# Two more pairs of a chunked state-space kernel transposed by DMA, and two stores issued by GpSimd

## The chip, the cores and the metric

The kernel runs on one core of a Trainium2 chip. The metric is the device time of one execution in microseconds; lower is better. The time before is the median of three runs. TensorE (PE in the profile), VectorE (DVE), ScalarE (ACT) and GpSimd (POOL) compute; SyncE (SP) only issues DMAs, and GpSimd and ScalarE can issue them too. Each engine works through its own instructions in order.

## The reference

Two stages, one behind the other. The first is a Mamba2-style scan over 4 batches, 8 heads and 768 positions, with head width 32 and state width 16, in chunks:

```python
L = np.exp(cum[:, :, :, None] - cum[:, :, None, :]) * causal
CB = np.einsum('bhin,bhjn->bhij', Cc, Bc)
y_intra = np.einsum('bhij,bhjd->bhid', CB * L, xc)
y_inter = np.einsum('bhin,bhnd->bhid', Cc, state) * decay_to_i
state = decay_full * state + sum_j(Bc x xc * decay_from_j)
```

Its result, as 3072 tokens of 256 features, goes through a gated feed-forward stage:

```python
gate = np.maximum(x @ w_gate, 0.0)      # 256 -> 1536
out = (gate * (x @ w_val)) @ w_out      # 1536 -> 256, float32
```

## The kernel before

The decays are folded into B and C: each position's B and C are multiplied by a factor (`fac`), so that within a chunk the product C·B already carries L, and only the causal mask is left. Chunks are 128 positions here, and two chunks of one batch with all 8 heads make a **pair**; there are 12 pairs (0 to 11). Two pairs make a **block** of 512 tokens for the feed-forward stage; the blocks of the outer loop are `b` = 0 to 5. While block b runs its feed-forward matmuls (`gv`, `gvh`, `fout`), the scan of later pairs is threaded between them: `P = 2b+2`, `Q = 2b+3`, `W = 2b+1`. The order on each engine is the order of the program text (`in_order` pins it), so what stands ahead of a waiting instruction on an engine, or behind it, can be read off the code.

For a pair p the steps are:

- `load(p)` or `held(p)`: SyncE loads C and B (`load_bc`, two DMAs each, L92) into `bcr`, and x (`load_x`, two DMAs, L100) into `xr`. `held` first writes one element with VectorE, which ties the load to VectorE's progress.
- `scale(p)`: B and C times `fac`, cast to bf16, on GpSimd, and `to_x(p)`: x cast to bf16 (`xb`, L318).
- A transpose of B and C, so that the state index n lies on the partitions. Pairs 0 to 5: scaled values go to `bs` (`scale_bc` L344, or `scale_one` L353 for one of B and C), `turn(p)` transposes them on TensorE (four matmuls against the identity, L389) into PSUM, and `tevac(p)` copies them out: B to `BT` on ScalarE, and C twice to `CT`, each time with the rows of half of the heads zeroed by `tmask` (L415 on VectorE). Pairs 6 to 11 (`NDMA = 6`): `scale_padded` writes B and C into one of three tiles `bz` (list `turned`, index p % 3), which were zeroed once, in eight slots of 128 columns; per chunk i, slot 4i is B, 4i+1 is C, and 4i+2 and 4i+3 are C with half of the heads left zero (L297, L303). One DMA transpose by SyncE (L306) then turns the whole tile into `TT`.
- `G(p)`: C·B for both chunks and all heads (L452, reading `BT` and `CT`); `G_rows` (L491) does so from `TT` for pairs 6 to 11. `gevac(p)`: two of the four quarters of the result leave PSUM through ScalarE (L464, L472) and get the causal mask from GpSimd (`affine_select`, L171); the rest is masked by VectorE (L475, L479).
- `inter(p, i)`: the carried state times C (L619, reading `CT` through `ct`); `Dm(p)`: the masked C·B times x (L630; for two pairs `Dm_two`, L678). `states(p)` (L569) and `states_two` (L693): B times x, summed over chunks; `spread` prepares it for `inter`.
- `yevac` writes the result to `yT`, which the feed-forward stage reads.

`foevac(b, ts)` (L811) copies a block's output to `ob` on ScalarE and stores it; every block's stores but the last ones are issued by SyncE (L814).

At the change, the program before reads as follows. End of block 0: `held(5)` (C, B and x of pair 5 on SyncE, L1064), the scan steps of pairs 2 and 3, `scale_one(4)` for B on GpSimd (L1117), the second store of block 0. Start of block 1 (L966): `load(6)`, `load(7)` on SyncE. Inside it: `states(4)` and `scale_one(4)` for C (L989); from f = 6 on `turn(4)`, `tevac(4)`, `scale(5)` (L1017); from f = 8 on `turn(5)`, `tevac(5)`, `scale(6)`, `load(8)` (L1021); then `inter(4)`, `fout(1, 0)`, `G(4)` with its masks, `Dm(4)`, `states(5)`, `G(5)`. Block 2 works on pairs 6 and 7 with `G_rows` and `Dm_two`, while GpSimd scales pairs 8 and 9.

Of the kernel before, what the change touches and what calls it, by code (L numbers as in the profile page):

```python
# [11 lines left out]
ALU = mybir.AluOpType  # L12
# [17 lines left out]
def kernel(  # L30
# [13 lines left out]
    nc = tc.nc  # L44

    NB, NH, S, D = x.shape
    N = B.shape[-1]
# [23 lines left out]
    NWIDE = 4  # L71
# [220 lines left out]
    def scale_padded(p, eng):  # L292

        b, c0, _ = place(p)
        z = turned[p % 3]
        f = fac[:, b, c0:c0 + 2].rearrange("s i j h -> s i (j h)")
        eng.tensor_tensor(  # L297
            out=z.rearrange("s (i k) (h n) -> s i (k h) n", k=4, n=N)[:, :, 0:2 * NH],
            in0=st[p]["bcr"].rearrange("s i j h n -> s i (j h) n"),
            in1=f.to_broadcast([128, 2, 2 * NH, N]), op=ALU.mult)  # L300
        parts = z.rearrange("s (i k) (q t n) -> s i k t q n", k=4, q=4, t=2)
        for t in range(2):
            eng.tensor_copy(out=parts[:, :, 2 + t, t], in_=parts[:, :, 1, t])  # L303
        st[p]["B"] = [z[:, 4 * i] for i in range(2)]
        tt = st[p]["TT"] = att.tile([128, 8, 128], BF16, tag="TT", name="TT", bufs=4)
        nc.sync.dma_start_transpose(out=tt, in_=z.rearrange("s k n -> s (k n)"))  # L306

    def new_bs(p):
        st[p]["bs"] = att.tile([128, 4, 128], BF16, tag="bs", name="bs", bufs=6)
# [107 lines left out]
    def ct(p, i, rows=slice(0, 128), t=None):  # L417
        if p < NWIDE:
            c = st[p]["CT"][rows, :, :, 64 * i:64 * i + 64]
        else:  # L420
            c = st[p]["CT"][rows, :, i]
        return c if t is None else c[:, t]

    def split(p, ap):

        return ap.rearrange("s t (r m) -> s t r m", r=2) if p < NWIDE else ap
# [17 lines left out]
    def G(p):  # L444
        s = st[p]
        if "gp" not in s:
            G_banks(p)
        g = s["gp"]
        for i in range(2):
            for q in range(4):  # L450
                r = slice(32 * q, 32 * q + 32)
                nc.tensor.matmul(  # L452
                    out=split(p, g[q][:, i]), lhsT=s["BT"][r, i], rhs=ct(p, i, r),
                    start=(i == 0), stop=True, tile_position=(32 * q, 0),
                    skip_group_check=True)
        s["gs"] = att.tile([128, 4, 4, 128], BF16, tag="gs", name="gs", bufs=2)
# [344 lines left out]
    def foevac(b, ts, o=None):  # L801
        last = b == NBLK - 1 and ts == 2
        if ts % 2 == 0 and not last:
            return
        ob = ffn.tile([128, 2, DM], FP32, tag="ob", name="ob", bufs=3)
        r0 = b * 512 + ts * 128
        if last:
            nc.scalar.copy(out=ob[:, 0], in_=fst["o"][:, 0])
            nc.scalar.dma_start(out=out[r0:r0 + 128, :], in_=ob[:, 0])
            return  # L810
        nc.scalar.copy(out=ob, in_=o or fst["o"])  # L811
        rows = out[r0 - 128:r0 + 128, :].rearrange("(i p) m -> p i m", p=128)
        for part in ((slice(0, 1), slice(1, 2)) if b in (2, 3) and ts == 3 else (slice(0, 2),)):
            nc.sync.dma_start(out=rows[:, part], in_=ob[:, part])  # L814


    B_, C_ = slice(0, 1), slice(1, 2)
# [89 lines left out]
    def turn(p):  # L907
        transp(p, 1)
        transp(p, 0)
# [53 lines left out]
    for b in range(NBLK):  # L963
        P, Q, W = 2 * b + 2, 2 * b + 3, 2 * b + 1
        more = P < NPAIR
        if b == 1:  # L966
            load(P + 2, nc.sync)
            load(P + 3, nc.sync)
        if b == 2:
            scale(Q, nc.gpsimd)  # L970
            load(Q + 2, nc.sync)

        nh = (4, 6, 8, 0)[min(b, 3)]
        for f in range(nh):
            if b == 0:
                continue
            turning = f == (3 if b == 1 else nh - 3)
            gvh_mm(b, f, 0)
            gvh_relu(b, f, 0)
            gvh_mul(b, f, 0)  # L980
            if b == 1 and f == 1:
                to_x(P, nc.scalar)
            if turning:
                inter(W, 0)
                inter(W, 1)
                Dm(W)
                if b == 1:
                    states(P)
                    scale_one(P, nc.gpsimd, 1)  # L989
                else:  # L990
                    states_two((P, Q))
                yevac(W, nc.scalar)
                if b == 1:
                    spread(P)
                else:
                    sums_two((P, Q))
# [4 lines left out]
        for f in range(nh, NF):  # L1001
            gv(b, f, b > 2 and f == 0)
            if b == 0:
                if f == 5:
                    over_sum(de_ps)
                if f == 7:
                    sevac(1, 1)
                if f == 9:
                    turn(P)
                    tevac(P, nc.scalar, nc.vector)  # L1010
                if f == 10:
                    held(Q, bc=False)
                if f == 11:
                    back(P)
                    backevac(P, nc.scalar)
            elif b == 1:
                if f == nh:  # L1017
                    turn(P)
                    tevac(P, nc.scalar, nc.vector)
                    scale(Q, nc.gpsimd)  # L1020
                if f == 8:  # L1021
                    turn(Q)
                    tevac(Q, nc.scalar, nc.vector)
                    scale(Q + 1, nc.gpsimd)
                    load(Q + 3, nc.sync)
            elif b == 2:
                if f == 9:
                    scale(Q + 2, nc.gpsimd)
                    load(Q + 3, nc.sync)
                    load(Q + 4, nc.sync)  # L1030
            elif b == 3:
                if f in (2, 6):
                    scale(P + 2 + f // 4, nc.gpsimd)
# [3 lines left out]
        if b == 0:  # L1037

            for third in range(3):
                fs = range(4 * third, 4 * third + 4)  # L1040
                fout(b, 0, fs)
                fout(b, 1, fs)
                if third == 0:
                    new_bc(Q + 1)
                    nc.vector.memset(st[Q + 1]["bcr"][0:1, 0, 0, 0, 0:1], 0.0)
                    load_bc(Q + 1, 0, nc.sync)
                    new_x(Q + 1)
                    for i in range(2):
                        load_x(Q + 1, i, nc.sync)
                    load_bc(Q + 1, 1, nc.sync)  # L1050
                    for n in range(1, NB):
                        nc.vector.reciprocal(fac[:, n, :, 0], fac[:, n, :, 1])
                if third == 0:
                    turn(Q)
                if third == 1:
                    G(P)
                    gevac(P)
                    tevac(Q, nc.scalar, nc.vector)
            foevac(b, 1)
            to_x(Q, nc.scalar)  # L1060
            fout(b, 2)
            state(P, 0)
            state(P, 1)
            held(Q + 2)  # L1064
            back(Q)
            backevac(Q, nc.vector)
            fout(b, 3, range(6))
            inter(P, 0)
            inter(P, 1)
        elif b == 1:  # L1070
            fout(b, 0)
            G(P)
            gevac(P)
            over_sum2(de)
            fout(b, 1)
            foevac(b, 1)
            fout(b, 2)
        elif more:
            ahead = (P + 2, Q + 2) if Q + 2 < NPAIR else ()
            fout(b, 0, range(9), True)  # L1080
            G_rows(P)
            opened = y_banks()
            inter_rows(P, opened)
            inter_rows(Q, opened)
            gevac(P)
            fout(b, 0, range(9, NF))
            fout(b, 1)
            first_two = fst["o"]
            fout(b, 2, range(1))
            G_rows(Q)  # L1090
            gevac(Q)
            foevac(b, 1, first_two)
            fout(b, 2, range(1, NF))
            fout(b, 3, range(8))
            Dm_two((P, Q))
            states_two(ahead)
            yevac_two((P, Q))
            sums_two(ahead)
            fout(b, 3, range(8, NF))
            foevac(b, 3)  # L1100
            continue
        else:
            fout(b, 0)
            fout(b, 1)
            foevac(b, 1)
            fout(b, 2)
            foevac(b, 2)
            fout_last(b)
            continue
        Dm(P)  # L1110
        states(Q)
        if b == 0:
            yevac(P, nc.vector)
            G(Q)
            gevac(Q, after={3: lambda: spread(Q)})
            new_bs(Q + 1)
            scale_one(Q + 1, nc.gpsimd, 0)  # L1117
        else:
            yevac(P, nc.scalar)
            G(Q)  # L1120
            spread(Q)
            gevac(Q)
# [34 lines left out]
```

## Time and profile before

| | us |
|---|---|
| median of three runs (122.37 to 123.28) | 122.76 |
| the profiled execution's own time | 122.67 |
| its span in the trace | 121.0 |

| engine | busy us | share of the span |
|---|---|---|
| TensorE, matmuls | 115.5 | 95% |
| VectorE | 89.0 | 74% |
| ScalarE | 74.3 | 61% |
| GpSimd | 51.5 | 43% |

The granted TensorE clock is 1.0 over the whole span. Where the profile's text gives times, they count from the start of the span. "L306" is line 306 of the kernel before. Names such as `TT<-bz` mean "writes TT, reads bz". SPq rows are SyncE's DMA issues: their length is the time in which SyncE was busy issuing, not the time of the transfer; the time from issue to landing is given separately. The waits shown in brackets are the idle time of an engine ahead of an instruction and who ended it.

### The profile page before, as it was taken

How to read it: one execution, taken by the hardware profiler on the slowest of the kernel's cores; microseconds unless marked ns; L12 is line 12 of the kernel's file. 1: busy time of each engine (PE TensorE's matmuls, PEld its weight loads, DVE VectorE, ACT ScalarE, POOL GpSimd, SP SyncE). 2: the span in 40 equal slices, each digit the busy share in tenths (PEclk: the TensorE clock that was granted, in tenths of full speed). 3: DMA queues.
4: the chain of work that ended last, by engine and by line, in shares of the span. 5: the costliest groups of instructions: out<-in, count | busy, mean ns of one | idle time of the engine just before them, and what ended most of it. 6: DMA issues, size and time to landing. Idle time of an engine off the chain costs nothing.

```text
span 121.0 us, 3322 instructions
## 1 busy us (share of the span) xinstructions
PE 115.5 (95%) x1231; PEld 74.8 (62%) x1238; DVE 89.0 (74%) x214; ACT 74.3 (61%) x161; POOL 51.5 (43%) x104
## 2 busy tenths in 40 slices
PE   7789999999999999999999999999999999999990
PEld 2245864577885477888487544578444677444790
DVE  5888888977999956899875687866778675678500
ACT  4166886843998744888734767525767445766340
POOL 6879999831705252857084363433400033000000
PEclk9999999999999999999999999999999999999999
DMA  3999999999989999899978799962200002200022
GB/s 67 208 172 162 201 186 188 207 141 130 161 99 170 125 105 131 106 202 182 115 138 136 80 107 152 197 127 78 95 5 0 0 0 92 87 0 0 0 87 87
DMA packets 80591, 13.69 MB, mean 113 GB/s; under 512 B 73424, under 2 KB 80576, under 8 KB 80576
## 3 DMA queue, kind: packets, MB, share of 16 engines
q1 hardware_dynamic: 73088, 10.54, 56.9%
q0 software_dynamic: 4080, 2.36, 14.0%
q10 hardware_dynamic: 3408, 0.59, 2.6%
q8 instruction: 9, 0.15, 0.5%
q14 instruction: 6, 0.05, 0.1%
HBM read 11.12 MB, written 3.15 MB: 118 GB/s over the span
## 4 chain that ended last, share of the span: by engine, by line
PE 89%; DVE 3%; DMA 3%; issue 1%; SPq 1%; ACT 0%; DVEq 0%
PE o L783 26%; PE gate L738 19%; PE val L738 19%; PE gv L753 13%; DMA bcr<-in_C_dram 3%; PE g L452 2%; PE g L491 2%; PE y L678 1%; PE y L630 1%; PE o L795 1%; DVE bs L344 1%; PE tp L389 1%; DVE gs L475 1%; PE y L619 1%; PE y L665 0%
## 5 line engine op out<-in xcount | busy, mean ns | idle before, releaser
L742 DVE TENSOR_TENSOR h<-r,val 128x512 bf16<-128x512 bf16 x54 | 36.7, 686 | 9.3 <-ACT r L741 6.4
L741 ACT ACTIVATE r<-gate 128x512 bf16<-128x512 f32 x54 | 32.3, 597 | 11.9 <-PE gate L738 10.9
L783 PE MATMUL o<-wo,h 128*128 128x256 bf16 x276 | 33.7, 273 | 0.0
L738 PE MATMUL gate<-yT,wg 128*128 128x512 bf16 x105 | 32.0, 379 | 0.2
L738 PE MATMUL val<-yT,wv 128*128 128x512 bf16 x105 | 31.5, 379 | 0.2
L783 PEld LDWEIGHTS <-h 128*128 128x128 bf16 x276 | 25.7, 98 | 5.6 <-issue 1.4
L171 POOL TENSOR_SCALAR_AFFINE_SELECT gs<-gs 128x512 bf16<-128x512 bf16 (+1 forms) x24 | 12.2, 531 | 25.3 <-ACT gs L464 25.3
L475 DVE TENSOR_TENSOR gs<-g,masks 128x512 bf16<-128x512 f32 x24 | 15.4, 684 | 6.3 <-PE g L491 2.8
L738 PEld LDWEIGHTS <-wv 128*128 128x128 bf16 x108 | 10.6, 98 | 12.5
L738 PEld LDWEIGHTS <-wg 128*128 128x128 bf16 x108 | 10.4, 98 | 11.1
L464 ACT CAST gs<-g 128x512 bf16<-128x512 f32 x12 | 7.0, 587 | 14.6 <-PE g L452 6.2
L763 DVE TENSOR_TENSOR h<-r,gv 128x256 bf16<-128x256 bf16 x36 | 13.9, 416 | 0.9 <-ACT r L760 0.7
L760 ACT ACTIVATE r<-gv 128x256 bf16<-128x256 f32 x36 | 13.7, 389 | 1.2
L753 PE MATMUL gv<-yT,wg 128*128 128x256 bf16 x72 | 13.9, 273 | 0.0
L753 PE MATMUL gv<-yT,wv 128*128 128x256 bf16 x72 | 13.9, 273 | 0.0
L297 POOL TENSOR_TENSOR bz<-bcr,fac 128x512 bf16<-128x512 f32 x6 | 6.3, 1058 | 9.1 <-DMA bcr<-in_B_dram 9.1
L811 ACT COPY ob<-o 128x512 f32<-128x512 f32 x11 | 6.5, 595 | 4.0 <-PE o L783 4.0
L318 ACT CAST yT<-y 128x512 bf16<-128x512 f32 (+1 forms) x9 | 4.6, 531 | 5.4 <-PE y L678 3.4
L753 PEld LDWEIGHTS <-wv 128*128 128x128 bf16 x72 | 7.0, 98 | 0.8
L753 PEld LDWEIGHTS <-wg 128*128 128x128 bf16 x72 | 6.8, 98 | 1.1 <-issue 0.2
L318 POOL CAST xb<-xr 128x512 bf16<-128x512 f32 (+1 forms) x9 | 5.3, 594 | 3.8 <-DMA xr<-in_x_dram 3.7
L318 DVE CAST yT<-y 128x256 bf16<-128x256 f32 (+1 forms) x7 | 3.7, 550 | 4.0 <-PE y L678 2.0
(119 smaller groups left out, 110.7 us busy)
## 6 DMA issues: line engine op xcount, KB each, us to landing
xr<-in_x_dram SPq DMA_DIRECT2D x23, 128.0 KB, 3.3
out_dram<-ob SPq DMA_DIRECT2D x9, 256.0 KB, 2.5
bcr<-in_B_dram SPq DMA_DIRECT2D x16, 64.0 KB, 3.0
bcr<-in_C_dram SPq DMA_DIRECT2D x16, 64.0 KB, 2.9
wg<-in_moe_w_gate_dram POOLq DMA_DIRECT2D x6, 128.0 KB, 4.8
wv<-in_moe_w_val_dram POOLq DMA_DIRECT2D x6, 128.0 KB, 5.0
wo<-in_moe_w_out_dram POOLq DMA_DIRECT2D x3, 256.0 KB, 7.1
out_dram<-ob SPq DMA_DIRECT2D x4, 128.0 KB, 2.4
```

What stands on the lines that cost most here:

```text
L171: nc.gpsimd.affine_select(out=dst, in_=dst, pattern=pattern, compare_op=ALU.is_ge, fill=0.0, base=0, channel_multiplier=-1)
L318: (eng.copy if eng is nc.scalar else eng.tensor_copy)(out=out, in_=in_)
L464: nc.scalar.copy(out=d[:, 0], in_=g[0])
L475: nc.vector.tensor_tensor(out=d[:, q], in0=g[q], in1=m, op=ALU.mult)
L738: nc.tensor.matmul(out=o, lhsT=w_tile(ws, f, k), rhs=yT[:, k, tk], start=(k == 0), stop=(k == 1), skip_group_check=True)
L741: nc.scalar.activation(r, g, AF.Relu)
L742: nc.vector.tensor_tensor(out=fst[b][:, f], in0=r, in1=v, op=ALU.mult)
L753: nc.tensor.matmul(out=gv_[:, j], lhsT=w_tile((wgs, wvs)[j], f, k), rhs=yT[:, k, tk], start=(k == 0 and not (early and j)), stop=(k == 1), ...
L760: nc.scalar.activation(r[:, 0:256], fst[b, f, u][:, 0], AF.Relu)
L763: nc.vector.tensor_tensor(out=fst[b][:, f, u * 256:(u + 1) * 256], in0=fst.pop((b, f, u, "r"))[:, 0:256], in1=fst.pop((b, f, u))[:, 1], op ...
L783: nc.tensor.matmul(out=o[:, ts % 2], lhsT=fst[b][:, f, ts * 128:(ts + 1) * 128], rhs=wo[:, f], start=(f == 0 and new), stop=(f == NF - 1), ...
L811: nc.scalar.copy(out=ob, in_=o or fst["o"])
```

## The change

Pairs 4 and 5 take the DMA way. A new function `scale_turned(p)` writes B and the two half-zero forms of C, scaled, straight into the padded tile (four GpSimd instructions, no plain C in slot 4i+1), and `turn_padded(p)`, split off from `scale_padded`, issues the DMA transpose. `ct` and `G` read `TT` for these pairs; their matmuls keep their shapes. The transposes, copies and `bs` tiles of the two pairs are gone.

The order of SyncE's queue changes. Before: C and B of pair 5, x of 5, a store, C and B of pair 6, x of 6, load of 7, transpose of 6. After: C and B of 5, transpose of 4, x of 5, C and B of 6, transpose of 5, x of 6, load of 7, transpose of 6. On GpSimd: the masks of pair 2, the first store of block 0, the masks of pair 3, `scale_turned(4)`, the second store of block 0, `scale_turned(5)`, `to_x(5)`, and then the scaling of pair 6 as before.

```diff
@@ scale_padded
         st[p]["B"] = [z[:, 4 * i] for i in range(2)]
+        turn_padded(p)
+
+    def scale_turned(p, eng):
+
+        b, c0, _ = place(p)
+        z = turned[p % 3]
+        dst = z.rearrange("s (i k) (q t n) -> s i k t q n", k=4, q=4, t=2)
+        src = st[p]["bcr"].rearrange("s i j (t q) n -> s i j t q n", t=2)
+        f = fac[:, b, c0:c0 + 2]
+        for j in range(2):
+            for t in range(2):
+                eng.tensor_tensor(
+                    out=dst[:, :, j * (2 + t), t], in0=src[:, :, j, t],
+                    in1=f[:, :, j, 4 * t:4 * t + 4].to_broadcast([128, 2, 4, N]), op=ALU.mult)
+        st[p]["B"] = [z[:, 4 * i] for i in range(2)]
+
+    def turn_padded(p):
         tt = st[p]["TT"] = att.tile([128, 8, 128], BF16, tag="TT", name="TT", bufs=4)
-        nc.sync.dma_start_transpose(out=tt, in_=z.rearrange("s k n -> s (k n)"))
+        nc.sync.dma_start_transpose(out=tt, in_=turned[p % 3].rearrange("s k n -> s (k n)"))
@@ ct
-            c = st[p]["CT"][rows, :, i]
+            c = st[p]["TT"][rows, 4 * i + 2:4 * i + 4]
@@ G
-                    out=split(p, g[q][:, i]), lhsT=s["BT"][r, i], rhs=ct(p, i, r),
+                    out=split(p, g[q][:, i]), rhs=ct(p, i, r),
+                    lhsT=s["BT"][r, i] if p < NWIDE else s["TT"][r, 4 * i],
@@ foevac
-            nc.sync.dma_start(out=rows[:, part], in_=ob[:, part])
+            (nc.sync if b else nc.gpsimd).dma_start(out=rows[:, part], in_=ob[:, part])
@@ the loop over blocks
         if b == 1:
-            load(P + 2, nc.sync)
+            new_bc(P + 2)
+            load_bc(P + 2, 1, nc.sync)
+            load_bc(P + 2, 0, nc.sync)
+            scale_turned(Q, nc.gpsimd)
+            turn_padded(Q)
+            new_x(P + 2)
+            for i in range(2):
+                load_x(P + 2, i, nc.sync)
             load(P + 3, nc.sync)
+            to_x(Q, nc.gpsimd)
...
                     states(P)
-                    scale_one(P, nc.gpsimd, 1)
...
             elif b == 1:
-                if f == nh:
-                    turn(P)
-                    tevac(P, nc.scalar, nc.vector)
-                    scale(Q, nc.gpsimd)
                 if f == 8:
-                    turn(Q)
-                    tevac(Q, nc.scalar, nc.vector)
                     scale(Q + 1, nc.gpsimd)
                     load(Q + 3, nc.sync)
...
-            held(Q + 2)
+            held(Q + 2, with_x=False)
...
-            new_bs(Q + 1)
-            scale_one(Q + 1, nc.gpsimd, 0)
+            scale_turned(Q + 1, nc.gpsimd)
+            turn_padded(Q + 1)
+            new_x(Q + 2)
+            for i in range(2):
+                load_x(Q + 2, i, nc.sync)
```

## The prediction

> **What bounds the kernel now.** I read the busy shares first, then the chain of waits, then the order of the SyncE queue and of GpSimd where the change falls, and last the DMA view. One profiled execution: span 121.0 us, its own time 122.67 us, so 1.67 us lie outside the span. The median of the three runs is 122.76 us, 0.09 above it. The runs reach from 122.37 to 123.28, so about 1% (1.2 us) is what a measurement tells from no change.
>
> ```profile
> PE 115.5 (95%) x1231; PEld 74.8 (62%) x1238; DVE 89.0 (74%) x214; ACT 74.3 (61%) x161; POOL 51.5 (43%) x104
> ```
> ```profile
> PE 89%; DVE 3%; DMA 3%; issue 1%; SPq 1%; ACT 0%; DVEq 0%
> PE o L783 26%; PE gate L738 19%; PE val L738 19%; PE gv L753 13%; DMA bcr<-in_C_dram 3%; PE g L452 2%; PE g L491 2%; PE y L678 1%; PE y L630 1%; PE o L795 1%; DVE bs L344 1%; PE tp L389 1%; DVE gs L475 1%; PE y L619 1%; PE y L665 0%
> ```
>
> The chain is TensorE almost throughout; ScalarE has 0% of it. So a microsecond off TensorE's stream is a microsecond off the end, as long as nothing that feeds it turns late. The second view to read is therefore what feeds it:
>
> ```profile
> DMA  3999999999989999899978799962200002200022
> ```
>
> The DMA engines are full until about two thirds of the span, and the change adds DMA work in that part.
>
> **What comes off TensorE.** The chain of waits of the stretch where pairs 4 and 5 are turned, and where their results are first read (start us, us, what):
>
> ```profile
> 37.81 0.22 PE tp L389 x4
> 39.76 0.22 PE tp L389 x4
> 42.57 0.22 PE y L619 x4
> ```
>
> The eight transposes stand on the chain with 0.22 + 0.22 = 0.44 us, between matmuls that follow without a gap. They go. The two copies on ScalarE and the four masked copies on VectorE that emptied them go too; the chain shows these engines hardly at all, so I cost their going at nothing, below and above. Matmuls of G and of the inter term for pairs 4 and 5 read TT in place of BT and CT with the same shapes: nothing. Without any new wait the kernel is at 122.67 - 0.44 = 122.23.
>
> **What is added to SyncE's queue.** Its rows before (start us, us, line, tile, count):
>
> ```profile
> 29.90 0.83 SPq L814 DMA_DIRECT2D out_dram<-ob  x1
> 30.83 1.19 SPq L92 DMA_DIRECT2D bcr<-in_C_dram  x2
> 32.07 1.41 SPq L92 DMA_DIRECT2D bcr<-in_B_dram  x2
> 33.52 2.52 SPq L100 DMA_DIRECT2D xr<-in_x_dram  x2
> 36.14 0.53 SPq L814 DMA_DIRECT2D out_dram<-ob  x1
> 36.77 1.18 SPq L92 DMA_DIRECT2D bcr<-in_C_dram  x2
> 38.00 1.28 SPq L92 DMA_DIRECT2D bcr<-in_B_dram  x2
> 39.38 1.38 SPq L100 DMA_DIRECT2D xr<-in_x_dram  x2
> 40.80 1.64 SPq L92 DMA_DIRECT2D bcr<-in_C_dram  x2
> 42.49 1.36 SPq L92 DMA_DIRECT2D bcr<-in_B_dram  x2
> 45.19 1.46 SPq L306 DMA_TRANSPOSE TT<-bz  x1
> 46.71 2.12 SPq L92 DMA_DIRECT2D bcr<-in_C_dram  x2
> 48.87 1.54 SPq L92 DMA_DIRECT2D bcr<-in_B_dram  x2
> 53.20 1.30 SPq L306 DMA_TRANSPOSE TT<-bz  x1
> 54.56 2.28 SPq L92 DMA_DIRECT2D bcr<-in_C_dram  x2
> ```
> ```profile
> L306 SPq DMA_TRANSPOSE TT<-bz x6: 1233/1442/1537, 45.2 to 77.1; - x6
> DMA to landing us min/median/max: 2.7/3.9/5.1
> ```
>
> SyncE issues one DMA after the other with no room between, so whatever is put into the queue moves every later load. I call the shift of the loads s and add it up to the B load of pair 9.
> - Issue: two transposes at the median 1.44 make +2.9; the two stores that leave took 0.83 + 0.53 = 1.36. Net +1.5.
> - New wait: the transpose of pair 4 waits for GpSimd's scaling, and x of pair 5, B and C of pair 6, the transpose of pair 5 and all behind them queue with it. SyncE gets there at 33.48 less 0.93 for the store, 32.55. GpSimd is done with the four scaling instructions at 33.38 (row below: the four instructions of the same size, 31.89 to 33.38). So +0.8.
> - Eased congestion: x of pair 5 took 2.52 where x of pair 6 took 1.38, 1.1 more with no transpose near. A pause of SyncE just ahead lets the engines catch up: between 0 and -1.1, and I take -1.1, since the pause stands right in front of it.
> - What a transpose leaves behind it: C and B after the transpose at 45.19 took 3.66 together; those of pairs 6 and 7 took 2.46 and 3.00. That is +0.9, and C behind the one at 53.20 shows the same. Two of these are 0 to 1.8. But the 1.1 at 33.52 says that such hold-ups come without transposes, so I take half of one, 0.45.
>
> Likeliest s = 1.5 + 0.8 - 1.1 + 0.45 = 1.65, with ends 0.4 (1.5 - 1.1) and 4.1 (1.5 + 0.8 + 1.8).
>
> The transposes' own landing is covered: that of pair 4 is issued at about 33.4 and at the longest landing, 5.1, is there at 38.5, ahead of its first reader at 42.57 less 0.44. That of pair 5, issued near 40 and landed by 45.1, is read by G(5), which stands between the two Dm rows below, after 47.0.
>
> **What is added to GpSimd.** Its rows (start, us, line, tile, count, [idle before and releaser]):
>
> ```profile
> 30.89 1.04 POOL L171 TENSOR_SCALAR_AFFINE_SELECT gs<-gs 128x512 bf16<-128x512 bf16 x2 [3.24 <-ACT gs L464]
> 31.89 1.49 POOL L353 TENSOR_TENSOR bs<-bcr,fac 128x128 bf16<-128x128 f32 x4
> 43.27 0.61 POOL L318 CAST xb<-xr 128x512 bf16<-128x512 f32 x1
> 45.18 1.00 POOL L171 TENSOR_SCALAR_AFFINE_SELECT gs<-gs 128x512 bf16<-128x512 bf16 x2 [1.29 <-ACT gs L464]
> 60.72 1.06 POOL L297 TENSOR_TENSOR bz<-bcr,fac 128x512 bf16<-128x512 f32 x1 [3.86 <-DMA bcr<-in_B_dram]
> 62.38 0.61 POOL L318 CAST xb<-xr 128x512 bf16<-128x512 f32 x1
> 62.95 1.01 POOL L171 TENSOR_SCALAR_AFFINE_SELECT gs<-gs 128x512 bf16<-128x512 bf16 x2
> 64.96 1.00 POOL L171 TENSOR_SCALAR_AFFINE_SELECT gs<-gs 128x512 bf16<-128x512 bf16 x2 [1.00 <-ACT gs L464]
> ```
> ```profile
> L153 POOL DMA_DIRECT2D wg<-in_moe_w_gate_dram x6 | 4.6, 774 | 0.3 <-POOL wg L225 0.3
> ```
>
> A store issued here is not in the trace; the nearest row is a weight load issued by GpSimd, 0.77 us. The first one falls into the 3.24 us of idle time before 30.89, the second behind the scaling of pair 4, in front of that of pair 5, whose data is what it waits for anyway. Both at nothing; were that cover gone, 0.77 us would go onto s, inside its upper end. B of pair 4 is ready after two of the four instructions, 32.7, as before, so the states of pair 4 do not move.
>
> **Where s meets TensorE.** GpSimd works in order, and behind the load waits stand the causal masks that the Dm matmuls read:
>
> ```profile
> 47.09 0.41 PE L630 MATMUL y<-gs,xb 128*32 128x128 bf16 x16
> 66.32 0.63 PE L678 MATMUL y<-gs,xb 128*32 128x128 bf16 x32
> ```
> ```profile
> DMA to landing us min/median/max: 3.0/3.1/3.2
> ```
>
> First place: x of pair 6 (landing line above: the pair of x loads issued at 39.38, whose second lands near 43.2) lets the cast start at 43.27, then 1.0 us of mask for pair 4. With s it ends at 43.27 + 0.61 + 1.0 + s = 44.9 + s, and Dm(4) wants it at 47.09 - 0.44 = 46.65: covered to s = 1.8. Second place: GpSimd stood 3.86 us waiting for B of pair 9; from 60.72 on it scales, copies, casts and masks without a pause until 63.96, then the second mask takes 1.0. That ends at 64.96 + s, and the Dm of pairs 6 and 7 wants it at 66.32 - 0.44 = 65.9: covered to s = 0.9. This is the tighter place. A stall at the first gives the second the same time more, so the larger of the two counts, not the sum: the uncovered part is s - 0.9.
>
> So the sum is 122.67 - 0.44 + (1.65 - 0.9) = 123.0.
>
> **A rule on the stores.** The DMA share by windows (last but one column; busy us of each engine before it):
>
> ```profile
> 36.80:45.20 8.40, 8.35 (x65) 4.95 (x64) 6.58 (x14) 5.53 (x12) 4.01 (x8) 1.00 1.04 140
> ```
>
> With a share of 1.04 the 16 engines themselves may set the pace, and not SyncE's issuing. Then moving the stores frees nothing: s = 1.65 + 1.36 = 3.0, uncovered 2.1, time 124.3. The Trainium skill, page "DMA: Bandwidth & Descriptors", section "Issuing engines are not separate DMA queues", says that DMAs started from the scalar, sync or gpsimd queue share the same 16 engines, and that spreading them over queues only saves time on the sequencer. The share agrees with that as far as it goes; that the rows behind the queue come at 0.6 us each whatever their bytes speaks for SyncE as the pace.
>
> **The rivals.**
> - Forecast: TensorE gains 0.44, the loads shift by 0.9 to 2.65, part of it is uncovered. 122.2 to 124.0, likeliest 123.0. Chance 0.52.
> - All covered: s at most 0.9, because the removed stores and the eased congestion pay for the transposes. 122.2, chance 0.18. For it: 1.5 - 1.1. Against it: one more wait on GpSimd.
> - Slower: the load stream is held up, and the Dm matmuls of pairs 6 and 7 wait for a mask behind B of pair 9. It decides for over 1% from s = 2.65. By the engines as the pace, 124.3 (chance 0.12); by hold-ups behind both transposes, up to s = 4.1, 125.4 (chance 0.14). For it speaks the DMA view of 45 to 53 us, where in 0.2 us slices the data stops for about 1.4 us after the transpose was issued:
>
> ```profile
> GB/s 119 103 102 100 125 183 214 201 202 241 261 266 58 0 0 3 6 10 10 9 210 293 198 145 141 123 124 70 62 59 56 92 120 118 127 153 150 168 151 139
> ```
>
> - Faster by over 1%: 1.2 us would have to go where the chain shows 0.44. I see no row for the rest. Chance 0.04.
> - That the change does not do what it says I leave out: the eight transposes are gone from TensorE's order in the changed program.
>
> **The numbers.** Faster by over 1% 0.04; within 1% 0.52 + 0.18 = 0.70; slower 0.26. Time 123.0, the likeliest case. The range starts at 122.0 (all covered, less a little scatter of the runs) and ends at 124.6: it takes in the engine-paced case and leaves out the worse half of the slower one and the faster one, 0.16 together.
>
> **What would show it.** Right: no tp rows on the chain between 36 and 42 us; SyncE reaching x of pair 6 later by 1 to 2 us than 39.38; GpSimd's scaling of pair 9 later than 60.72 by about s, and an idle time of TensorE of under a microsecond before the Dm of pairs 6 and 7, released by GpSimd. Wrong: no TensorE idle there (all covered); one of 2 us or more, or one already at Dm(4) (held up); or a wait at states of pair 4 or at the inter term of pair 4, which would mean that the scaling or the new transpose itself is late.

## The result and the profile after

The changed kernel takes 124.31 us (median of six runs, 123.67 to 126.42), the kernel before beside it 122.75 us (six runs, 122.37 to 123.37). The ratio is 1.0105, with a 95% interval of 1.0076 to 1.0134: slower by about 1%. (The ratio leaves out executions more than 1.5% above the fastest of their kernel, here two of the six, and the medians do not, so the medians lie further apart.) The forecast was 123.0 with a range of 122.0 to 124.6. The time is inside the range, near the figure of the case that was called slower, and on the edge of what had been called "within 1%".

The profiled execution of the changed kernel took 123.67 us, the fastest of its six and 1.00 more than that of before (122.67); its span is 122.0 us. First the busy shares and the chain of waits of the page after:

```profile
PE 116.8 (96%) x1223; PEld 75.1 (62%) x1230; DVE 88.1 (72%) x210; ACT 73.6 (60%) x159; POOL 53.3 (44%) x108
```
```profile
PE 69%; DMA 10%; POOL 7%; SPq 6%; DVE 3%; issue 2%; ACT 1%; POOLq 0%; ACTq 0%; DVEq 0%
PE o L801 17%; PE gate L756 16%; PE val L756 15%; PE gv L771 7%; DMA bcr<-in_B_dram 5%; DMA xr<-in_x_dram 5%; PE w L200 4%; SPq L92 3%; POOL gs L171 3%; SPq L323 2%; POOL bz L297 2%; PE y L696 1%; PE g L469 1%; PE g L509 1%; PE o L813 1%
```

TensorE's share of the chain fell from 89% to 69%. DMA, GpSimd and SyncE together now hold 23%, where the chain of before had 4% of DMA and SyncE and no GpSimd. TensorE's busy sum looks no smaller (116.8 against 115.5), although it has eight instructions fewer: its ends are modelled, and a matmul that waits inside a group counts as busy. So the sum can't show the gain; the starts of groups can.

TensorE's rows at the three places that matter, after (start us, us; the bracket is the idle time ahead). The first row is the first gate matmul of block 0; the same row starts at 16.17 in the kernel before:

```profile
16.14 0.38 PE L756 MATMUL gate<-yT,wg 128*128 128x512 bf16 x1
...
47.21 0.71 PE L648 MATMUL y<-gs,xb 128*32 128x128 bf16 x16 [0.52 <-POOL gs L171]
...
66.74 1.21 PE L696 MATMUL y<-gs,xb 128*32 128x128 bf16 x32
```

Read against the gate row, Dm of pair 4 starts at 31.07, before at 47.09 - 16.17 = 30.92. Eight transposes are gone in between (0.44), so it waited 0.15 + 0.44 = 0.59 (the bracket names 0.52 of it), and the group is 0.30 longer (0.71 against 0.41) because it waits inside as well: 0.89 in all. Dm of pairs 6 and 7 is 0.58 longer (1.21 against 0.63). 0.89 + 0.58 - 0.44 = 1.03, and that is the whole of the 1.00. Behind it nothing more is lost: from the first gate matmul of block 3 to TensorE's end it is 50.73 us in both traces.

GpSimd's rows that release these matmuls, after:

```profile
43.36 1.06 POOL L297 TENSOR_TENSOR bz<-bcr,fac 128x512 bf16<-128x512 f32 x1 [2.35 <-DMA bcr<-in_B_dram]
...
45.95 0.61 POOL L335 CAST xb<-xr 128x512 bf16<-128x512 f32 x1 [0.95 <-DMA xr<-in_x_dram]
46.52 1.00 POOL L171 TENSOR_SCALAR_AFFINE_SELECT gs<-gs 128x512 bf16<-128x512 bf16 x2
...
63.28 1.06 POOL L297 TENSOR_TENSOR bz<-bcr,fac 128x512 bf16<-128x512 f32 x1 [5.50 <-DMA bcr<-in_B_dram]
...
64.90 0.61 POOL L335 CAST xb<-xr 128x512 bf16<-128x512 f32 x1
65.47 1.97 POOL L171 TENSOR_SCALAR_AFFINE_SELECT gs<-gs 128x512 bf16<-128x512 bf16 x4
```

The cast of x of pair 6 starts at 45.95 in place of 43.27 (2.68 later), the scaling of pair 9 at 63.28 in place of 60.72 (2.56 later). In both cases the masks stand behind a wait for a load, in an engine that has nothing else to do. The chain of the second place shows it in a line, after:

```profile
60.07 3.01 DMA bcr<-in_B_dram
...
63.28 1.07 POOL bz L297
...
64.90 0.61 POOL xb L335
65.52 1.94 POOL gs L171 x4
...
67.49 0.43 PE y L696 x17
```

SyncE's queue, after, to be read against the rows that the prediction shows (L323 is the transpose):

```profile
28.38 3.93 SPq L92 DMA_DIRECT2D bcr<-in_C_dram  x4
32.35 1.30 SPq L92 DMA_DIRECT2D bcr<-in_B_dram  x2
33.75 2.76 SPq L323 DMA_TRANSPOSE TT<-bz  x1
36.61 1.15 SPq L100 DMA_DIRECT2D xr<-in_x_dram  x2
37.81 1.75 SPq L92 DMA_DIRECT2D bcr<-in_C_dram  x2
39.60 1.20 SPq L92 DMA_DIRECT2D bcr<-in_B_dram  x2
40.91 1.48 SPq L323 DMA_TRANSPOSE TT<-bz  x1
42.44 1.21 SPq L100 DMA_DIRECT2D xr<-in_x_dram  x2
```

Before, the first of B of pair 5 was issued at 32.07, with a store ahead of it; now at 32.35, without one. The store that left gave no time back: the four C rows take 3.93 us where C, store and C took 28.34 to 32.02. Then the transpose of pair 4 takes 2.76 and x of pair 5 only 1.15, where x of pair 5 took 2.52 before. The hold-up at 33.5 us did not go; it moved from the x load onto the transpose.

### The profile page after: what moved, and what is told of

Read it like the earlier page. It is cut to its first block, busy times and chain, and to the rows that moved or that the text cites. A ratio compares the mean times of both kernels' runs of the same rounds, so it can differ in the third digit from the quotient of the medians.

```text
span 122.0 us, 3306 instructions
## 1 busy us (share of the span) xinstructions
PE 116.8 (96%) x1223; PEld 75.1 (62%) x1230; DVE 88.1 (72%) x210; ACT 73.6 (60%) x159; POOL 53.3 (44%) x108
## 4 chain that ended last, share of the span: by engine, by line
PE 69%; DMA 10%; POOL 7%; SPq 6%; DVE 3%; issue 2%; ACT 1%; POOLq 0%; ACTq 0%; DVEq 0%
PE o L801 17%; PE gate L756 16%; PE val L756 15%; PE gv L771 7%; DMA bcr<-in_B_dram 5%; DMA xr<-in_x_dram 5%; PE w L200 4%; SPq L92 3%; POOL gs L171 3%; SPq L323 2%; POOL bz L297 2%; PE y L696 1%; PE g L469 1%; PE g L509 1%; PE o L813 1%
```

## The experiments

The theory was: the two transposes and what they do to SyncE's queue delay the loads, and through GpSimd's order the masks. Rivals: the 16 DMA engines set the pace whatever SyncE issues; the stores on GpSimd cost; GpSimd's order does not matter. All ratios are to the kernel before on the same chip, with the 95% interval. There is one trace of each kernel, and the load stream of one execution scatters, as will be seen; so ratios carry more than a single trace. The rows come from several chips (the kernel before has medians of 122.53 to 123.13 beside them), and the change itself was timed only in its six executions; so compare ratios, not medians.

| kernel | median us | ratio | interval |
|---|---|---|---|
| the change | 124.31 | 1.0105 | 1.0076 to 1.0134 |
| its transposes left out | 122.77 | 1.0007 | 0.9977 to 1.0038 |
| its stores back on SyncE | 125.78 | 1.0235 | 1.0185 to 1.0285 |
| x of pair 6 ahead of the transpose of pair 5 | 124.84 | 1.0203 | 1.0150 to 1.0256 |
| masks earlier in GpSimd's order | 123.43 | 1.0067 | 1.0013 to 1.0121 |
| pair 4 alone | 123.14 | 0.9983 | 0.9933 to 1.0034 |
| pair 5 alone, measured again | 123.31 | 1.0033 | 0.9999 to 1.0068 |
| before, with the stores on GpSimd | 123.07 | 1.0003 | 0.9969 to 1.0038 |
| loads of pairs 8 and 9 earlier | 126.49 | 1.0245 | 1.0181 to 1.0309 |
| the change without block 0's stores | 123.61 | 1.0046 | 1.0010 to 1.0083 |
| both pairs, all masks placed | 123.41 | 1.0035 | 1.0006 to 1.0064 |
| pair 4 alone, masks placed | 122.62 | 0.9992 | 0.9970 to 1.0014 |

**The transposes left out.**

```diff
+        if p < NDMA:
+            st[p]["TT"] = turned[p % 3]
+            return
         tt = st[p]["TT"] = att.tile([128, 8, 128], BF16, tag="TT", name="TT", bufs=4)
```

> As the changed kernel, but the two new DMA transposes are left out: G and inter of pairs 4 and 5 read the untransposed padded tile, so their part of the output is not the reference's. Theory (the transposes push the load stream back, and GpSimd, working in order, hands that on to the masks): the loads come earlier than in the kernel before, GpSimd's scaling of pair 9 starts at about 59.5 us (60.7 before, 63.3 changed), no wait of TensorE at either Dm, time 122.3 +- 0.4. Rival, the GpSimd side (four scaling instructions, stores issued there) costs it: time stays at 124.0 to 124.5.

The rise is gone: 1.0007 against 1.0105, and the intervals don't touch. So without the two transposes the change costs nothing, but it gains nothing either: the 0.4 us under the kernel before that was expected did not show. SyncE's rows of this kernel at the place where the transpose of pair 4 stood follow (this execution began 2.0 us later on TensorE, its first gate matmul is at 18.17):

```profile
34.93 1.78 SPq L92 DMA_DIRECT2D bcr<-in_B_dram  x2
36.81 2.24 SPq L100 DMA_DIRECT2D xr<-in_x_dram  x2
```

Without any transpose in that stretch x of pair 5 is again held up, for 2.24 us. The hold-up belongs to the place. Measured from the first gate matmul, the scaling of pair 9 starts at 45.9 us here, against 44.6 before and 47.1 after: of the 2.6 us of shift this trace gives half to the transposes. The other half it does not explain, and it is enough for a wait. Dm of pair 4 has none, as expected, but Dm of pairs 6 and 7 has one, where none was expected:

```profile
67.97 0.30 PE L699 MATMUL y<-gs,xb 128*32 128x128 bf16 x8
68.46 0.82 PE L699 MATMUL y<-gs,xb 128*32 128x128 bf16 x24 [0.19 <-POOL gs L171]
```

From first to last the group takes 1.31 us, against 0.63 in the kernel before.

**The stores back on SyncE.**

```diff
-            (nc.sync if b else nc.gpsimd).dma_start(out=rows[:, part], in_=ob[:, part])
+            nc.sync.dma_start(out=rows[:, part], in_=ob[:, part])
```

> As the changed kernel, but block 0's two stores are issued by SyncE again. Theory (SyncE's issuing sets the pace of the loads): the loads come later by the 1.4 us that the two stores took there, scaling of pair 9 at about 64.5 us, time 125.3. Rival, the 16 DMA engines set the pace: nothing moves, 124.3. Rival, the stores on GpSimd are themselves what costs: faster than the changed kernel, 123.5 or less.

Slower, 1.0235. In this trace the scaling of pair 9 starts 48.1 us after the first gate matmul, 1.0 later than in the changed kernel, and Dm of pair 4 waits 1.04 for its mask where it waited 0.52. The stores on GpSimd are not what costs. The direction is that of the first theory (loads later by 1.4 us); by this kernel the two stores do cost something in SyncE's queue.

**x of pair 6 ahead of the transpose of pair 5.**

```diff
             scale_turned(Q, nc.gpsimd)
-            turn_padded(Q)
             new_x(P + 2)
             for i in range(2):
                 load_x(P + 2, i, nc.sync)
+            turn_padded(Q)
```

> As the changed kernel, but SyncE issues x of pair 6 ahead of the transpose of pair 5. Theory (of the two places where a late load meets TensorE the larger counts, not the sum): the wait at Dm of pair 4 goes away (x of pair 6 lands 1.5 us earlier), the one at Dm of pairs 6 and 7 grows by as much, because B of pair 9 lands as late as before; time 124.3 +- 0.4. Rival, the place at Dm of pair 4 is what costs: 123.4.

TensorE's rows of the two Dm places:

```profile
48.63 0.41 PE L648 MATMUL y<-gs,xb 128*32 128x128 bf16 x16
...
68.55 0.60 PE L696 MATMUL y<-gs,xb 128*32 128x128 bf16 x8 [0.25 <-POOL gs L171]
69.50 0.82 PE L696 MATMUL y<-gs,xb 128*32 128x128 bf16 x24 [0.36 <-POOL gs L171]
```

The first wait is gone and the second has grown, as expected. So taking the earlier of two stalls away gains nothing while the load stream, the same SyncE queue, is as late at the later one. But the kernel is also slower than the change, by about 1% (1.0203, intervals that do not touch), and 124.84 us lies above the 124.3 +- 0.4 that was expected. Its trace shows 0.36 us lost at the sums of pairs 6 and 7, which wait for the cast of pair 7; the rest of this 1% stays open.

**Masks earlier.** The cast of pair 6 goes behind the masks of pair 4, and the scaling of pair 9 behind the masks of pair 6:

```diff
                 if f == 8:
-                    scale(Q + 1, nc.gpsimd)
+                    scale_padded(Q + 1, nc.gpsimd)
...
             elif b == 2:
-                if f == 9:
-                    scale(Q + 2, nc.gpsimd)
-                    load(Q + 3, nc.sync)
-                    load(Q + 4, nc.sync)
+                pass
...
             gevac(P)
+            to_x(Q + 1, nc.gpsimd)
...
             gevac(P)
+            if b == 2:
+                scale(Q + 2, nc.gpsimd)
+                load(Q + 3, nc.sync)
+                load(Q + 4, nc.sync)
```

> As the changed kernel, but in GpSimd's order the masks of pair 4 stand ahead of the cast of x of pair 6, and the masks of pair 6 ahead of the scaling of pair 9; SyncE's order is the same. Theory (the late loads cost only because the masks queue behind them on GpSimd): no wait at Dm of pair 4; at Dm of pairs 6 and 7 the masks of pair 7 still come behind the scaling of pair 9, which ends near 65.5, so TensorE waits some 0.6 us; time 122.9 +- 0.4. Rival, late loads hold TensorE in another way (transposed tiles, states): 124.0 or more.

GpSimd's rows:

```profile
64.01 1.06 POOL L297 TENSOR_TENSOR bz<-bcr,fac 128x512 bf16<-128x512 f32 x1
...
66.17 1.00 POOL L171 TENSOR_SCALAR_AFFINE_SELECT gs<-gs 128x512 bf16<-128x512 bf16 x2
```

More of the rise is left than was expected, 1.0067 (123.43 us, expected 122.9 +- 0.4), and its interval overlaps that of the change, so by the times alone a gain is not shown. In the trace no wait is left at Dm of pair 4. What is left has three parts. The masks of pair 7 still stand behind the scaling and the cast of pair 9 (second row), and Dm of pairs 6 and 7 is 0.48 too long (1.11 against 0.63). The sums of pairs 6 and 7 lose 0.46, waiting for the cast of pair 7. And 0.51 was lost in block 0 already, ahead of the edit: there TensorE was held up, at the end by a weight load that landed at 26.01, in code that all these kernels share.

**Each pair alone.** The other pair goes back to TensorE (`turn`, `tevac`), the stores stay on GpSimd:

```diff
-            scale_turned(Q, nc.gpsimd)
-            turn_padded(Q)
+            new_bs(Q)
+            scale_bc(Q, nc.gpsimd)
...
                 if f == 8:
+                    turn(Q)
+                    tevac(Q, nc.scalar, nc.vector)
```

> Pair 4 by DMA, pair 5 back on TensorE, the stores as changed. Theory (each transpose in SyncE's queue moves the loads behind it by its own issue, and the moved loads are what TensorE waits for): one transpose of 1.5 us less, so the shift falls from 2.56 us to about 1.1, B of pair 9 lets its scaling start near 61.8, TensorE waits at the Dm of pairs 6 and 7 by 0.2 us or less, time 122.6 to 123.2. Rival (the wait of SyncE for GpSimd ahead of the transpose of pair 4, with what it holds up behind it, is what costs, and the second transpose is covered): like the changed kernel, 124.0 to 124.6.

> Pair 5 by DMA, pair 4 back on TensorE, the stores as changed. Theory (each transpose moves the loads by its own issue): shift about 1.0, time 122.6 to 123.2, as with pair 4 alone. Rival (the wait of SyncE for GpSimd at the transpose of pair 4 costs): like the kernel before or under it by the 0.2 us of four transposes, 122.2 to 122.6, and clearly faster than pair 4 alone.

> Pair 5 alone by DMA once more, since the first look gave too few comparable times. If each transpose delays the loads by its own 1.5 us at most: ratio 0.997 to 1.004, like pair 4 alone. If pair 5's transpose is the one that costs: 1.007 to 1.014.

Pair 4 alone is no slower than before (0.9983). Pair 5 alone gave 122.60, 124.55 and 124.83 us at first and a profiled execution of 584.55 (last section), from which nothing follows; measured again it gave 1.0033. Neither comes near the 1.0105 of both together, so by the times the rise is not one transpose's. The traces do not bear out the theory that each transpose moves the loads by its own issue, some 1.1 us: the scaling of pair 9 starts 46.7 us after the first gate matmul in both, 2.1 later than before. In the profiled execution of pair 4 alone, 123.67 us, that already exceeds the cover (the room at Dm of pairs 6 and 7, 0.9 us in the prediction and 1.1 where four transposes stay on TensorE), and Dm of pairs 6 and 7 takes 1.65 us from first to last, against 0.63:

```profile
66.20 0.46 PE L698 MATMUL y<-gs,xb 128*32 128x128 bf16 x8
67.03 0.82 PE L698 MATMUL y<-gs,xb 128*32 128x128 bf16 x24 [0.36 <-POOL gs L171]
```

Its ten times lie in two groups, 122.20 to 122.61 (five) and 123.67 to 124.57 (five). That the second group is this wait, present in some executions and absent in others, is argued from the one trace, not shown.

**The kernel before, with the stores on GpSimd.**

```diff
-            nc.sync.dma_start(out=rows[:, part], in_=ob[:, part])
+            (nc.sync if b else nc.gpsimd).dma_start(out=rows[:, part], in_=ob[:, part])
```

> The kernel before, with only block 0's two stores moved to GpSimd. Theory (SyncE's issuing paces the loads): the loads behind the stores come up to 1.4 us earlier, the scaling of pair 9 starts at 59.3 to 60.0 in place of 60.72; the time stays, 122.3 to 122.7, since TensorE waits for nothing there. Rival (the 16 engines pace the loads): the scaling of pair 9 stays at 60.5 to 60.9, time the same.

The time stays, as both theories expected. SyncE's rows:

```profile
31.99 1.34 SPq L92 DMA_DIRECT2D bcr<-in_B_dram  x2
33.43 3.74 SPq L100 DMA_DIRECT2D xr<-in_x_dram  x2
37.26 1.32 SPq L92 DMA_DIRECT2D bcr<-in_C_dram  x2
```

The loads behind the stores did not come 1.4 us earlier. SyncE is at x of pair 5 at 33.43 with the first store elsewhere, and was at 33.52 with it; then x takes 3.74. The scaling of pair 9 starts at 61.55, 45.8 us after the first gate matmul, 1.2 later than before. TensorE does not wait for it: with its transposes in place it reads the masks later. This trace contradicts the theory that moving stores off SyncE frees the queue by their issue time; the kernel with the stores back on SyncE speaks for it. What the stores do to the loads is not settled by these two.

**The change without block 0's stores.**

```diff
-            (nc.sync if b else nc.gpsimd).dma_start(out=rows[:, part], in_=ob[:, part])
+            if b:
+                nc.sync.dma_start(out=rows[:, part], in_=ob[:, part])
```

> The changed kernel with block 0's two stores (256 KB each) left out altogether: SyncE's queue is the same instruction for instruction, only the 16 engines have less to move. Theory now (the engines' own pace and their hold-ups set the load stream, so the stores cost it wherever they are issued): the loads behind come earlier, the scaling of pair 9 starts 45.0 to 46.0 us after the first gate matmul of block 0 (47.1 in the changed kernel, 44.6 in the kernel before), ratio to the kernel before 0.995 to 1.004. Rival (SyncE's issuing and its wait at the transposes set it): 46.8 to 47.5, ratio 1.007 to 1.014 as for the changed kernel.

The trace speaks for the rival: SyncE reaches the transpose of pair 4 at 33.80, which then takes 2.38, and the scaling of pair 9 starts 63.80 - 16.05 = 47.8 us after the first gate matmul, no earlier than after. The ratio, 1.0046, lies between the two expectations. So 512 KB less for the engines do not bring the loads forward in this trace; whether they take something off the time, the overlapping intervals (to 1.0083 here, from 1.0076 there) leave open.

**The loads of pairs 8 and 9 earlier.**

```diff
                 if f == 8:
-                    scale(Q + 1, nc.gpsimd)
                     load(Q + 3, nc.sync)
+                    load(Q + 4, nc.sync)
...
             gevac(P)
+            scale(Q + 1, nc.gpsimd)
...
             scale(Q, nc.gpsimd)
-            load(Q + 2, nc.sync)
```

> The changed kernel with the loads of pairs 8 and 9 issued ahead of the transpose of pair 6 and of block 1's stores, and GpSimd's scaling and cast of pair 6 placed behind the masks of pair 4. Theory (what costs is load data that GpSimd waits for in front of masks): no load wait of GpSimd in front of the masks of pairs 4, 6 and 7, Dm of pair 4 and of pairs 6 and 7 as in the kernel before, time 122.1 to 122.6. Rival (the room is missing elsewhere: the transposes of pairs 6 and 7 now come late for G, or the sums of pairs 6 and 7): a new wait of TensorE at G of pairs 6 or 7, 123.0 or more.

The rival: the first transpose of block 2's pairs now stands behind six more pairs of load DMAs in the same queue. TensorE's rows:

```profile
64.84 0.30 PE L683 MATMUL y<-TT,Sn 32*64 32x128 bf16 x8 [1.85 <-DMA TT<-bz]
67.66 0.65 PE L509 MATMUL g<-TT 32*64 32x256 bf16 x16
71.02 0.63 PE L696 MATMUL y<-gs,xb 128*32 128x128 bf16 x32
```

The wait has gone from a load to the transpose of pair 7, and Dm of pairs 6 and 7 starts at 71.02 in place of 66.74. Not all of this is the rival's. 1.46 us were lost in block 0, ahead of the edit, where the transposes of pair 3 waited for a late load of B. And behind the wait shown, from 66.5 to 69.5 us, the granted clock reads 0.50, and the `o` matmuls there are slower (19 of them take 2.85 us, 2.25 in the changed kernel); over this stretch that adds 1.56 us. In one queue, whatever is put ahead puts something else back.

**All masks placed.** In addition to the earlier masks, the masks of pair 7 go between the scaling and the cast of pair 9:

```diff
             if b == 2:
-                scale(Q + 2, nc.gpsimd)
+                scale_padded(Q + 2, nc.gpsimd)
...
             gevac(Q)
+            if b == 2:
+                to_x(Q + 2, nc.gpsimd)
```

> Both pairs by DMA, masks of pair 4 ahead of the cast of pair 6, masks of pair 6 ahead of the scaling of pair 9, and masks of pair 7 between that scaling and the cast of pair 9. Theory (the delayed loads cost only through GpSimd's order): Dm of pairs 6 and 7 at most 0.2 us late, ratio 0.998 to 1.003. Rival (another place comes late, the sums of pairs 6 and 7 behind the cast of pair 7 or those of pairs 8 and 9 behind the cast of pair 9): 1.004 to 1.010.

> Pair 4 alone by DMA, with the masks of pairs 6 and 7 set around the scaling of pair 9 in the same way. Theory: no wait at the Dm of pairs 6 and 7, four transposes less on TensorE, ratio 0.995 to 0.999. Rival (scatter of the load stream hits elsewhere): 1.000 to 1.006.

TensorE's rows with both pairs by DMA:

```profile
46.67 0.41 PE L648 MATMUL y<-gs,xb 128*32 128x128 bf16 x16
...
65.95 0.63 PE L696 MATMUL y<-gs,xb 128*32 128x128 bf16 x32
```

Both Dm waits are gone with the order of GpSimd alone. The first row starts 46.67 - 16.20 = 30.47 us after the first gate matmul, 0.45 earlier than before: the eight transposes' 0.44, seen at last. The profiled execution took 122.48 us. Over all executions the ratio is 1.0035, a third of the rise, with an interval below that of the change; the expectation (0.998 to 1.003) is just missed. Its other times reach from 122.53 to 124.78 (and one is 151.16), and without their traces it stays open what holds them up. Pair 4 alone with masks placed ends at 0.9992, like before (0.995 to 0.999 was expected). None of these versions is faster than the kernel before.

**Shift and stall, trace by trace.** In the kernels that leave the scaling of pair 9 at its place, the prediction's rule can be tried on every trace. The shift is how much later that scaling starts than in the kernel before, from the first gate matmul. The cover is 1.36 us from the rows of before, less what the transposes that are gone take off TensorE (0.22 a pair). The stall is how much later block 3's first gate matmul comes, also from that of block 0, with that gain added. (The change's 2.59 is the 2.56 above, which counts from the start of the spans.) All in us:

| kernel | shift | cover | shift less cover | stall |
|---|---|---|---|---|
| before, with the stores on GpSimd | 1.22 | 1.36 | none | 0.01 |
| its transposes left out | 1.39 | 0.92 | 0.47 | 0.77 |
| pair 4 alone | 2.11 | 1.14 | 0.97 | 1.02 |
| pair 5 alone, measured again | 2.15 | 1.14 | 1.01 | 0.91 |
| the change | 2.59 | 0.92 | 1.67 | 1.48 |
| x of pair 6 ahead of the transpose | 2.82 | 0.92 | 1.90 | 1.83 |
| without block 0's stores | 3.20 | 0.92 | 2.28 | 2.06 |
| its stores back on SyncE | 3.55 | 0.92 | 2.63 | 2.40 |

The stall follows the shift within 0.3 us in all of them, whatever made the loads late. What does not follow is the shift from the number of transposes alone.

## Why the prediction came out as it did

- **TensorE gains 0.44.** Right in size. No TensorE transposes stand on the chain between 36 and 42 us any more (it runs through SyncE, DMA and GpSimd there), and where no wait hides the gain, it is 0.45.
- **The net issue time, +1.5.** Mis-sized in both parts. The transposes took 2.76 and 1.48, not 1.44 each. The credit of 0.83 for the first store did not show at this place: nine kernels without it on SyncE, whose first gate matmul comes at the same time within 0.4 us, are done with B of pair 5 between 33.33 and 34.44, and with it this is 33.48 (before) and 33.68 (stores put back). SyncE's issue rows there stretch to fill the time.
- **The wait for GpSimd, +0.8.** It did not come. SyncE was expected at 32.55, arrived at 33.65 (32.35 + 1.30), and the scaling of pair 4 ended at 33.58. This error and the store's cancel, which is luck.
- **Eased congestion, -1.1.** This is the step that failed. The hold-up of about a microsecond at 33.5 us did not ease; the instruction that stands there pays it: x of pair 5 with 2.52 before and 2.24 without transposes, the transpose with 2.76 after and 2.38 to 2.74 in seven other kernels. Where SyncE did pause there, 0.67 us in the kernel with the earlier loads, the transpose took 1.33, but x behind it 2.09 in place of 1.15. Without this term s is 1.5 + 0.8 + 0.45 = 2.75; 2.56 was measured, against the 1.65 that was taken. It lies inside the ends 0.4 and 4.1.
- **What a transpose leaves behind it, +0.45.** Not separated from the rest. C and B behind the first transpose took 1.75 + 1.20 = 2.95, before 2.46; those behind the second 1.30 + 2.41 = 3.71, before 3.00. Put down to the transposes, that would be 1.20.
- **Where s meets TensorE.** Right. Covered to 1.8 at Dm of pair 4: 2.68 - 1.8 = 0.88, measured 0.89. Covered to 0.9 at Dm of pairs 6 and 7: 2.56 - 0.9 = 1.66 for both together, measured 0.89 + 0.58 = 1.47, while the sum of both would be 2.54. That the larger counts agrees with the kernel with x of pair 6 moved ahead, and the rule with eight traces (table above). With the measured s the prediction's own sum gives 122.67 - 0.44 + 1.66 = 123.9 for the profiled execution, which took 123.67.
- **The stores on GpSimd at nothing.** Right for GpSimd: they took 0.78 and 0.75, each ahead of a longer wait for something else (2.25 and 2.74), and putting them back on SyncE made the kernel slower still.
- **The engines as the pace, 124.3.** The figure is that of the median, but its mechanism is borne out only in part. That moving the stores frees nothing agrees with the kernel before with its stores on GpSimd. Against it stand the stores put back (1.0235) and the trace without stores, in which fewer bytes brought the loads no earlier. The Trainium skill, page "DMA: Bandwidth & Descriptors", section "Issuing engines are not separate DMA queues", calls the time saved by spreading the starts usually small relative to the DMA itself. Here the two stores on SyncE instead of GpSimd went with about 1.3% (1.0235 against 1.0105) in one pair of kernels and with nothing in the other (1.0003), where TensorE did not wait for the loads.
- **The signs.** SyncE reached x of pair 6 at 42.44, 3.06 later than 39.38 and not 1 to 2. The wait of TensorE at Dm of pairs 6 and 7 stayed under a microsecond, as it should if the forecast was right. But there is a wait at Dm of pair 4 too, and that was named as a sign of the rival, the load stream held up. With s = 2.56, where 2.65 was to decide for that rival, the outcome lies between the two.
- **The time.** Of the 1.3 us between 123.0 and 124.31, 0.67 is in the profiled execution (s larger by 0.91, the stalls 0.2 shorter than the sum makes them); the other 0.64 is what the median lies above that execution. Before, it was 0.08 (122.75 and 122.67). A kernel whose loads arrive without room scatters upward with them; that this is the cause here was not shown. That 124.31 is inside the range is in part luck: the forecast's own case ended at 124.0, and the range went on to 124.6 for the engines as the pace, whose mechanism is borne out only in part. (What the range leaves out adds up to 0.14 + 0.04 = 0.18 by the prediction's own chances, not 0.16.)

What stays open: half of the 2.56 us. Two traces in which pairs 4 and 5 have no DMA transpose keep about half of it (1.4 and 1.2), and one transpose, of either pair, comes with 2.1. The two have the stores on GpSimd in common, but without stores the shift is 3.2, and with them on SyncE 3.5. So it is not known which part of the stores' move is behind it, or whether it is scatter of one execution. Scatter there is: two kernels lost 0.5 and 1.5 us in block 0, ahead of their edits.

## What to carry to other kernels

Work moved from a full engine to a DMA queue is not free when the same queue carries the loads: count its issue time at the congested place, where the instruction that stands there pays the hold-up, and do not book a pause in the queue as relief. Look for the engine that runs in order between the loads and the bottleneck; here the cover at two places, 1.8 and 0.9 us, read off from the trace of before, gave the loss within 0.2 us once the shift was known (within 0.3 in seven other traces). Placing what must be on time ahead of what waits for loads took out two thirds of the loss, without touching the queue.

## What the runs showed of the hardware

TensorE's speed in the first microseconds differs between executions of unchanged code. The warm-up matmuls (L200), in the kernel before, in the changed kernel and in the one without transposes:

```profile
4.07 0.67 PE L200 MATMUL w<-const-bfloat16-1.0 128*128 128x512 bf16 x3
7.85 0.61 PE L200 MATMUL w<-const-bfloat16-1.0 128*128 128x512 bf16 x2
```
```profile
4.35 1.14 PE L200 MATMUL w<-const-bfloat16-1.0 128*128 128x512 bf16 x3
7.81 0.61 PE L200 MATMUL w<-const-bfloat16-1.0 128*128 128x512 bf16 x2
```
```profile
4.35 1.14 PE L200 MATMUL w<-const-bfloat16-1.0 128*128 128x512 bf16 x3
8.78 1.03 PE L200 MATMUL w<-const-bfloat16-1.0 128*128 128x512 bf16 x2
```

Three of them take 0.67 or 1.14 us, and two 0.61 or 1.03: TensorE becomes fast before 4 us, before 8, or only later, and in the last case everything behind is 2.0 us late. The Trainium skill, page "TensorE: Matmul & The Clock Gate", section "Part 1: The HAM clock gate", says that TensorE starts throttled and is released after a busy window of about 3.4 us, and that the windows run free of the kernel's start. The first two cases agree with that. The third is later than one window explains: a `gv` matmul at 12.54 still took 0.42 us, where the same row takes 0.27 in the kernel before, 11.7 us after the first matmul at 0.83; whether gaps between its matmuls are why is not shown. It follows that two profiles are compared from a common row, not from the span's start.

The profile of the execution of 584.55 us (pair 5 alone, the first time) has TensorE slow almost throughout, while the granted clock reads 1.000:

```profile
core 0: 582.8 us, clock 1.000
```
```profile
L803 PE MATMUL o<-wo,h 128*128 128x256 bf16 x276 | 164.1, 918 | 0.0
```

The same group takes 273 ns a matmul in the changed kernel. The Trainium skill, page "TensorE: Matmul & The Clock Gate", section "Seeing it yourself", warns that the clock events in traces have been seen to be unreliable, and the throttle stuck at a quarter for 50 us and more. A clock of 1.000 is therefore no proof of a full clock; the duration of a known matmul is.
